# Attention values two units at a time, masks added by VectorE for half the batches, and a 64-row tail padded to 128 rows

## The chip, the cores and the metric

The kernel runs on one core of a Trainium2 chip. The metric is the device time of one execution in microseconds (us); lower is better. Each figure for a version is the median of several executions.

## The reference, cut to what matters

Three blocks follow each other, all in float32, on 4 batches of 576 positions and 512 features (8 heads of 64).

```python
scores = scale * np.matmul(q, k.transpose(0, 1, 3, 2))      # 4 x 8 x 576 x 576, D = 64
# heads 0-3: rel in [0, 32); heads 4-7: rel in [0, 128) and rel % 4 == 0
scores = np.where(masks, scores, -1e9); attn = softmax(scores)
x = (attn @ v) as (B, S, 512)
xk = mu_k * x + (1 - mu_k) * x_prev;  xr = mu_r * x + (1 - mu_r) * x_prev
x = sigmoid(xr @ w_r) * ((relu(xk @ w_k) ** 2) @ w_v)        # 512 -> 1024 -> 512
h = relu(x.T @ w_tok1) @ w_tok2                              # over positions: 576 -> 256 -> 576
u = x + h.T
out = u + relu(u @ w_ch1) @ w_ch2                            # 512 -> 1536 -> 512
```

## The kernel before, in words

**Attention.** The host cuts queries into blocks of 64 and gives each block the 96 keys that its window can reach (heads 4 to 7 are regrouped by position modulo 4, so that their window is one of 32 again). A unit is four such blocks, each for a pair of heads; a batch has 9 units, and there are 36. `attend` (line 542) does one unit. TensorE first writes the four masks (0 or -1e30, bf16) into a PSUM bank by one matmul with an identity (128x384), then adds four score matmuls (128x96, float32) on top. VectorE takes the negated maximum of each row, ScalarE makes the four exponentials from the bank, VectorE sums, inverts and scales them; TensorE transposes the four blocks, and one engine copies the result to `pt`. Then TensorE multiplies by the values: 8 matmuls of 96x64 by 96x64 that write 64 rows by 64 columns each, in the two halves of the array in turn. `nc.burst` (line 225) keeps these 8 together in the order. The result is copied to `xT`, where batch b lies in slots `xt` 4(b%3) to 4(b%3)+3.

**Gated block.** Six chunks of 384 positions. For each, `prep` makes the mixed inputs (high and low float32r parts, in `z` 0 to 3), `keys` and `mix` do 8 slices of the 1024 hidden features, and `receptance` the gate. A product of two float32 matrices is three float32r matmuls (`mm3`: high x high, high x low, low x high). The chunks' results are the tiles `x2`, 18 of 128 positions. A batch has four and a half such tiles; tiles 8 and 17 hold the last 64 positions of two batches, one in rows 0 to 63 and one in rows 64 to 127.

**Token mix.** `tokens_in(b)` (line 817) goes over the five tiles of a batch (`tiles_of`, line 807): it splits each into high and low (ScalarE or VectorE copies, VectorE subtracts) and multiplies by the weights `t1[kt]`, 6 matmuls of 512 columns per tile. For the fifth tile only the 64 rows of this batch are split and used, so its six matmuls have 64 rows: 24 in all. `t1[4]` holds the last 64 rows of `w_tok1` twice, once in each half of the rows. `tokens_out` multiplies by `t2` and adds to `u`. The channel mix (`middle`, `result`) ends the kernel.

**Weights.** `weight` (line 480) loads float64 words, and ScalarE and VectorE turn them into high and low parts: one pass of ScalarE, three of VectorE, then a copy and a subtraction. `t1`, `t2` and the first four slices of `w_ch1` go by turns through the two raw buffers `xt` 4 and 5 and the two work buffers `xt` 6 and 7 (`raw_b`, `tmp_b`); everything later goes through `wr` 0 to 2.

**Order.** No engine's order is written by hand. `Plan` records every operation, works out what it depends on, gives each a due time (`order`, line 280: the place of the matmuls in program order, counted back through what feeds them) and lists the operations by a schedule with costs per form. Line 392 issues them all, so every row of the profile bears this line, and rows are told apart by tiles: a tile bears the name of its slot (`at`, `x`, `xt`, `wk`, `wr`, `wv`, `z`, `y`, `cst`) without its number, `bank` is a PSUM bank. All DMAs are issued by SyncE (SP), in one order. Attention of batches 1 to 3 lies beside the gated block: `beside` (line 729) deals its units over the slices.

Of the kernel before, what the change touches and what calls it, by code (L numbers as in the profile page):

```python
# [10 lines left out]
F32R = mybir.dt.float32r  # L11
# [41 lines left out]
FIRST = [sum(TILES[:c]) for c in range(len(CHUNKS))]  # L53
CH = 512
NEG = -1.0e30

SLOTS = dict(
    cst=[160], xt=[584] * 12, x2=[2048] * 2 + [1024] * 5, at=[3536, 784, 1216],
# [347 lines left out]
def tile_model(nc, banks, units, cst, mu, w_k, w_v, w_r, w_t1, w_t2, w_c1, w_c2, outT):  # L406
    memory = {k: [Slot(f"{k}{i}", n) for i, n in enumerate(v)] for k, v in SLOTS.items()}

    def f(view):
        return view.bitcast(F32)  # L410
# [10 lines left out]
    def cut(name, numbers, size, count=None):  # L421

        out = []
        for n in numbers:
            out += [(name, n, size * i) for i in range(SLOTS[name][n] // size)]
        return out[:count]

    def ring(*places):
        return Ring(at, sum((p if isinstance(p, list) else [p] for p in places), []))
# [19 lines left out]
    def split(raw, hi, lo):  # L449
        copy(hi, raw)  # L450
        combine(lo, raw, f(hi), ALU.subtract)

    def rows(n):
        return slice(128 * n, 128 * n + 128)
# [6 lines left out]
    def pair(place, shape):  # L461

        name, number, offset = place
        n = int(np.prod(shape))
        return at(place, shape, F32R), at((name, number, offset + n), shape, F32R)
# [11 lines left out]

        return words(w).rearrange("(k p) c -> p k c", p=128)[:, :, 2 * n * m:2 * n * m + 2 * n]

    def weight(srcs, hi, lo, raw_ring, tmp_ring):  # L480

        shape = tuple(hi.shape[1:])
        n = int(np.prod(shape))  # L490
        flat = raw_ring.tile(2 * n, dtype=U32)
        for part, src in srcs:
            dst = flat[part]
            if len(src.shape) == 3:
                dst = dst.split(src.shape[1], src.shape[2])
            nc.sync.dma_start(out=dst, in_=src)
            if raw_ring is raw_a:
                nc.early[len(nc.ops) - 1] = 6
        raw = flat.split(n, 2)
        low, h = raw[:, :, 0], raw[:, :, 1]  # L500
        t = tmp_ring.tile(n)
        b, half = t.bitcast(U32), t.bitcast(U16)
        v = nc.vector
        nc.scalar.activation(out=t, in_=f(h), func=AF.Copy, scale=2.0 ** -112)
        v.tensor_scalar(out=h, in0=b, scalar1=3, scalar2=None, op0=ALU.logical_shift_left)
        v.scalar_tensor_tensor(
            out=b, in0=b, scalar=0x80000000, in1=h, op0=ALU.bitwise_and, op1=ALU.bitwise_or
        )
        v.scalar_tensor_tensor(
            out=half, in0=low, scalar=2.0 ** -29, in1=half, op0=ALU.mult, op1=ALU.add  # L510
        )
        if len(shape) == 2:
            t = t.split(*shape)
        split(t, hi, lo)
# [27 lines left out]
    def attend(i, s_ring, t_ring, x_ring):  # L542

        b, runs = UNITS[i]
        unit, vs = unit_r.tile(UQ + UK), v_r.tile(NBLK, 2, D)[:KB]
        values = units[i][:KB, UQ + UK:].rearrange("p (a b c) -> p a b c", a=NBLK, b=2)
        for out, in_ in ((unit, units[i][:, :UQ + UK]), (vs, values)):
            nc.sync.dma_start(out=out, in_=in_)
            nc.early[len(nc.ops) - 1] = {0: 30, 1: -45}.get(b, 0)
        blocks, o = [], UQ  # L550
        for p, j0, n in runs:
            if j0 == 0:
                nc.gpsimd.memset(out=xT[b, p][:, 0:1], constant=0.0)
            blocks += [(p, j0 + j, unit[:, o + QB * j:o + QB * j + KB]) for j in range(n)]
            o += QB * n + W
        sp, sm, st = s_ring.tile(NBLK, KB), sm_r.tile(NBLK, KB), st_r.tile(4, NBLK)
        row = ROWS[i % len(RUNS)]
        nc.tensor.matmul(out=sp, lhsT=ident_h, rhs=masks[:, row:row + NBLK, :], start=True, stop=False)
        for n, (p, j, ks) in enumerate(blocks):
            qs = unit[:, 2 * QB * n:2 * QB * n + 2 * QB]  # L560
            nc.tensor.matmul(out=sp[:, n, :], lhsT=qs, rhs=ks, start=False, stop=n == NBLK - 1)
            if b:
                nc.early[len(nc.ops) - 1] = -0.5 * n
        scale = 1.0 / np.sqrt(D)
        nc.vector.tensor_reduce(
            out=st[:, 0, :], in_=sp, axis=mybir.AxisListType.X, op=ALU.max, negate=True
        )
        if b == 0 and i % 2:
            nc.vector.tensor_tensor(out=sm, in0=sp, in1=st[:, 0, :].wide(KB), op=ALU.add)
            nc.scalar.activation(out=sm, in_=sm, func=AF.Exp, scale=scale)  # L570
            nc.vector.tensor_reduce(out=st[:, 2, :], in_=sm, axis=mybir.AxisListType.X, op=ALU.add)
        else:
            nc.either(
                ("vector", "tensor_scalar", dict(
                    out=st[:, 1, :], in0=st[:, 0, :], scalar1=scale, scalar2=None, op0=ALU.mult)),
                ("scalar", "activation", dict(out=st[:, 1, :], in_=st[:, 0, :], func=AF.Copy, scale=scale)),
            )
            for j in range(NBLK):
                nc.scalar.activation(
                    out=sm[:, j, :], in_=sp[:, j, :], func=AF.Exp, scale=scale,  # L580
                    bias=st[:, 1, j:j + 1], accum_out=st[:, 2, j:j + 1],
                )
        nc.either(
            ("vector", "tensor_scalar_add", dict(out=st[:, 2, :], in0=st[:, 2, :], scalar1=1e-9)),
            ("scalar", "activation", dict(out=st[:, 2, :], in_=st[:, 2, :], func=AF.Copy, bias=1e-9)),
        )
        nc.vector.reciprocal(out=st[:, 3, :], in_=st[:, 2, :])
        combine(sm, sm, st[:, 3, :].wide(KB), ALU.mult)
        tp, pt = t_ring.tile(NBLK, 2 * QB)[:KB], pt_r.tile(NBLK, 2 * QB)[:KB]
        for j in range(NBLK):  # L590
            nc.tensor.transpose(out=tp[:, j, :], in_=sm[:, j, :], identity=ident)
        copy(pt, tp)
        xp = x_ring.tile(QB * NBLK)
        start = len(nc.ops)
        for j in range(NBLK):
            for hh in range(2):
                r = slice(64 * hh, 64 * hh + 64)
                nc.tensor.matmul(
                    out=xp[r, QB * j:QB * j + QB], lhsT=vs[:, j, hh, :], rhs=pt[:, j, r],
                    start=True, stop=True,  # L600
                )
        nc.burst(start)
        o = 0
        for p, j0, n in runs:
            x, t, end = xT[b, p][:, 1:], QB * j0, QB * (j0 + n)
            if p < 2:
                copy(x[:, t:end], xp[:, o:o + end - t])
                o += end - t
                continue
            x = x.split(S // 4, 4).swap()  # L610
            while t < end:
                c, k = divmod(t, S // 4)
                m = min(end - t, S // 4 - k)
                copy(x[:, c, k:k + m], xp[:, o:o + m])
                t, o = t + m, o + m
# [108 lines left out]

    s_ring, t_ring, x_ring = psum(0, 4), psum(1), psum(2)
    unit_r = ring([("at", 0, (UQ + UK) * i) for i in range(2)])
    v_r = ring([("at", 0, 2 * (UQ + UK) + UV * i) for i in range(3)])
    beside = {}
    for n, (lo, hi) in enumerate(([0, 20], [20, 42], [42, 68])):
        for i in range(n_units):  # L730
# [35 lines left out]
            attend(h, s_ring, t_ring, x_ring)  # L766


    t1 = [pair(p, (HID,)) for p in cut("at", (1, 2), 512) + [("at", 0, 4 * S), ("at", 0, 4 * S + 512)]]
    t2 = [pair(p, (S,)) for p in cut("at", (0,), 2 * S, 2)]  # L770
    raw_b, tmp_b = ring(cut("xt", (4, 5), 512)), ring(cut("xt", (6, 7), 512))
    for k in range(4):
        weight([(everything, words(w_t1)[rows(k), :])], *t1[k], raw_b, tmp_b)
    tail = words(w_t1)[512:576, :]
    weight([(slice(0, 64), tail), (slice(64, 128), tail)], *t1[4], raw_b, tmp_b)
    for k in range(2):
        for n in range(3):
            cs = slice(192 * n, 192 * n + 192)
# [27 lines left out]

    def tiles_of(b):
        base, odd = 9 * (b // 2), b % 2
        out = [(base + 4 * odd + i, slice(0, 128), i) for i in range(4)]
        return out + [(base + 8, slice(64 * odd, 64 * odd + 64), 4)]  # L810

    for m in range(4):
        weight_1(m)
    hid = {}
    hp_r, x2p_r, up_r = psum(0, 1, 2, 3), psum(4, 5), psum(6, 7)

    def tokens_in(b):
        hp = [hp_r.tile(C) for _ in range(2)]
        for n, (t, r, kt) in enumerate(tiles_of(b)):
            h, l = x2h_r.tile(C, dtype=F32R), x2l_r.tile(C, dtype=F32R)  # L820
            split(x2[t][r], h[r], l[r])
            for m in range(2):
                mm3(hp[m], t1[kt][0][r, rows(m)], t1[kt][1][r, rows(m)], h[r], l[r], n == 0, n == 4)
        hid[b] = []
        for m in range(2):
            h, l = (hid_r.tile(C, dtype=F32R) for _ in range(2))
            nc.scalar.activation(out=h, in_=hp[m], func=AF.Relu)
            nc.vector.scalar_tensor_tensor(
                out=l, in0=hp[m], scalar=0.0, in1=f(h), op0=ALU.max, op1=ALU.subtract
            )  # L830
            hid[b].append((h, l))
# [189 lines left out]
```

## Time and profile before

| what | value |
|---|---|
| time, median of 3 runs | 734.55 us (733.45 to 735.19) |
| the profiled execution's own time | 732.79 us |
| its span, first to last instruction | 731.0 us |
| TensorE matmuls (PE) busy | 715.6 us, 98% of the span |
| VectorE (DVE) busy | 404.7 us, 55% |
| ScalarE (ACT) busy | 287.1 us, 39% |
| mean granted TensorE clock | 0.989 of full |
| moved by DMA | 53.84 MB, 74 GB/s |

PE is busy nearly all the time, but a matmul's busy time overlaps the next one's, so what a matmul costs is read from the distance between the starts of neighbours, not from its own duration. A float32 matmul counts as two rows of the trace (two passes), a float32r or bf16 one and a transpose as one.

### The profile page before, as it was taken

How to read it: one execution, taken by the hardware profiler on the slowest of the kernel's cores; microseconds unless marked ns; L12 is line 12 of the kernel's file. 1: busy time of each engine (PE TensorE's matmuls, PEld its weight loads, DVE VectorE, ACT ScalarE, POOL GpSimd, SP SyncE). 2: the span in 40 equal slices, each digit the busy share in tenths (PEclk: the TensorE clock that was granted, in tenths of full speed). 3: DMA queues.
4: the chain of work that ended last, by engine and by line, in shares of the span. 5: the costliest groups of instructions: out<-in, count | busy, mean ns of one | idle time of the engine just before them, and what ended most of it. 6: DMA issues, size and time to landing. Idle time of an engine off the chain costs nothing.

```text
span 731.0 us, 10615 instructions
## 1 busy us (share of the span) xinstructions
PE 715.6 (98%) x4124; PEld 604.6 (83%) x4124; DVE 404.7 (55%) x917; ACT 287.1 (39%) x803; POOL 1.2 (0%) x20
## 2 busy tenths in 40 slices
PE   7699999999999999999999999999999999999998
PEld 6578888888888888988878888888888888888897
DVE  6898898387477388786788898132114112211121
ACT  5776775356244354464466543120112011011110
POOL 0000000000000000000000000000000000000000
PEclk9799999999999999999999999999999999999999
DMA  8946632214122100203321342001000000100010
GB/s 293 323 156 225 196 132 81 67 52 144 47 68 70 46 16 22 73 30 105 98 81 54 96 127 76 1 0 58 1 0 23 35 1 1 57 1 0 1 59 30
DMA packets 26082, 53.84 MB, mean 74 GB/s; under 512 B 2480, under 2 KB 10032, under 8 KB 26032
## 3 DMA queue, kind: packets, MB, share of 16 engines
q1 hardware_dynamic: 26032, 53.17, 22.9%
q8 instruction: 32, 0.52, 0.3%
q14 instruction: 18, 0.15, 0.1%
HBM read 48.44 MB, written 4.72 MB: 73 GB/s over the span
## 4 chain that ended last, share of the span: by engine, by line
PE 95%; DMA 4%; SPq 0%; issue 0%; DVE 0%
PE bank L392 95%; DMA at<-units 2%; DMA wr<-units 1%; DMA wv<-units 1%; SPq L392 0%; DVE z L392 0%
## 5 line engine op out<-in xcount | busy, mean ns | idle before, releaser
L392 PE MATMUL bank<-z,wk 128*128 128x384 f32 (+2 forms) x816 | 196.4, 358 | 0.0
L392 DVE SCALAR_TENSOR_TENSOR z<-bank,z 128x512 fp32r<-128x512 f32 (+2 forms) x116 | 70.4, 607 | 222.3 <-ACT z L392 221.5
L392 ACT ACTIVATE z<-bank 128x512 fp32r<-128x512 f32 (+3 forms) x123 | 65.0, 529 | 285.3 <-PE bank L392 284.3
L392 PEld LDWEIGHTS bank<-z,wk 128*128 128x128 f32 x816 | 146.9, 188 | 15.1 <-ACT x L392 0.3
L392 PE MATMUL bank<-wv,z 128*128 128x512 f32 x432 | 128.9, 405 | 0.0
L392 PE MATMUL bank<-z,x 128*128 128x512 f32 (+1 forms) x540 | 120.2, 371 | 0.0
L392 PEld LDWEIGHTS bank<-z,x 128*128 128x128 f32 x540 | 94.9, 188 | 18.7
L392 PEld LDWEIGHTS bank<-wv,z 128*128 128x128 f32 x432 | 78.3, 189 | 13.8
L392 PE MATMUL bank<-z,at 128*128 128x512 f32 (+2 forms) x300 | 76.9, 388 | 0.0
L392 PE MATMUL bank<-wr,z 128*128 128x512 f32 x216 | 62.8, 406 | 0.0
L392 PEld LDWEIGHTS bank<-z,at 128*128 128x128 f32 (+1 forms) x300 | 52.6, 188 | 11.3 <-issue 1.3
L392 PE MATMUL bank<-at 128*128 128x96 f32 (+1 forms) x252 | 46.3, 284 | 11.0 <-DMA at<-cst 4.9
L392 ACT ACTIVATE at<-bank,at 128x96 f32<-128x96 f32 x128 | 42.4, 340 | 23.7 <-PE bank L392 11.6
L392 DVE TENSOR_TENSOR z<-z,z 128x384 fp32r<-128x384 f32 x88 | 48.1, 554 | 5.8 <-ACT z L392 2.6
L392 PE MATMUL bank<-xt,wk 128*128 128x512 f32 (+2 forms) x176 | 45.2, 387 | 0.0
L392 PEld LDWEIGHTS bank<-wr,z 128*128 128x128 f32 x216 | 39.2, 189 | 6.6
L392 PEld LDWEIGHTS bank<-at 128*128 128x128 f32 x216 | 35.3, 195 | 8.0 <-DMA at<-units 4.1
L392 PE MATMUL bank<-at,z 128*128 128x288 f32 x192 | 35.9, 306 | 0.0
L392 PEld LDWEIGHTS bank<-xt,wk 128*128 128x128 f32 x176 | 30.5, 192 | 6.1
L392 ACT ACTIVATE z<-z 128x384 fp32r<-128x384 f32 x57 | 29.5, 522 | 14.3 <-DVE z L392 8.3
L392 ACT ACTIVATE x<-bank 96x512 f32<-96x512 f32 (+1 forms) x41 | 24.2, 594 | 27.1 <-PE bank L392 26.9
L392 PEld LDWEIGHTS bank<-at,z 128*128 128x128 f32 x192 | 29.7, 188 | 4.0 <-issue 1.8
(106 smaller groups left out, 787.2 us busy)
## 6 DMA issues: line engine op xcount, KB each, us to landing
at<-units SPq DMA_DIRECT2D x27, 416.0 KB, 3.7
wr<-w_c SPq DMA_DIRECT2D x20, 512.0 KB, 3.6
at<-units SPq DMA_DIRECT2D x27, 192.0 KB, 2.6
x<-w_k SPq DMA_DIRECT2D x4, 1024.0 KB, 6.9
x<-w_v SPq DMA_DIRECT2D x4, 1024.0 KB, 7.0
wv<-units SPq DMA_DIRECT2D x8, 416.0 KB, 6.6
outT<-z SPq DMA_DIRECT2D x9, 256.0 KB, 2.0
x<-w_r SPq DMA_DIRECT2D x4, 512.0 KB, 3.6
```

The source lines that it names most:

```text
L392: call(kw["out"], kw["constant"]) if method == "memset" else call(**kw)
```

## The change

Three edits and what they need.

1. For batches 2 and 3 (18 of the 36 units) the mask matmul is gone. The four score matmuls open their own sums, VectorE adds the mask while it moves the scores from the bank to the tile `sm`, and maximum and exponentials read `sm`.
2. The value matmuls of batches 1 to 3 are done for two units in one burst of 16 (the ninth unit of a batch stays alone): `attend` puts a unit on the list `waiting`, and `weigh` does what waits and copies it out by `place`. The ring of value tiles has a fourth place (`y`).
3. The fifth tile of a batch is used with all its 128 rows. The last 64 rows of `w_tok1` are prepared twice: `t1[4]` has them in rows 0 to 63 and zeros below, `t1[5]` (in `z512[8]`, which lies in slot `z` 2) the other way round; GpSimd (POOL) writes the zeros into the raw words. The tile is split once for both batches and its parts stay in `wr` 3.

```diff
+MASKED = 2
+TOGETHER = 2
...
-    def weight(srcs, hi, lo, raw_ring, tmp_ring):
+    def weight(srcs, hi, lo, raw_ring, tmp_ring, zero=None):
...
+        if zero is not None:
+            nc.gpsimd.memset(out=f(flat[zero]), constant=0.0)
...
-        nc.tensor.matmul(out=sp, lhsT=ident_h, rhs=masks[:, row:row + NBLK, :], start=True, stop=False)
+        mask = masks[:, row:row + NBLK, :]
+        by_pe = b < MASKED
+        if by_pe:
+            nc.tensor.matmul(out=sp, lhsT=ident_h, rhs=mask, start=True, stop=False)
...
-            nc.tensor.matmul(out=sp[:, n, :], lhsT=qs, rhs=ks, start=False, stop=n == NBLK - 1)
+            nc.tensor.matmul(out=sp[:, n, :], lhsT=qs, rhs=ks, start=not by_pe, stop=n == NBLK - 1 or not by_pe)
...
+        if not by_pe:
+            nc.vector.tensor_tensor(out=sm, in0=sp, in1=mask, op=ALU.add)
+            sp = sm
...
-        xp = x_ring.tile(QB * NBLK)
+        waiting.append((runs, b, vs, pt))
+        if b == 0 or len(waiting) == TOGETHER or (i + 1) % len(RUNS) == 0:
+            weigh(x_ring.tile(2, QB * NBLK))
+    def weigh(xps):
         start = len(nc.ops)
...
+        for n, (_, _, vs, pt) in enumerate(waiting):
+            for j in range(NBLK):
...
         nc.burst(start)
+        for n, (runs, b, _, _) in enumerate(waiting):
+            place(runs, b, xps[:, n, :])
+        waiting.clear()
...
-    v_r = ring([("at", 0, 2 * (UQ + UK) + UV * i) for i in range(3)])
+    v_r = ring([("at", 0, 2 * (UQ + UK) + UV * i) for i in range(3)], ("y", 0, 0))
...
-    weight([(slice(0, 64), tail), (slice(64, 128), tail)], *t1[4], raw_b, tmp_b)
+    halves = [slice(0, 64), slice(64, 128)]
+    for odd in range(2):
+        weight([(halves[odd], tail)], *t1[4 + odd], raw_b, tmp_b, zero=halves[1 - odd])
...
-        out = [(base + 4 * odd + i, slice(0, 128), i) for i in range(4)]
-        return out + [(base + 8, slice(64 * odd, 64 * odd + 64), 4)]
+        return [(base + 4 * odd + i, i) for i in range(4)] + [(base + 8, 4 + odd)]
...
-            h, l = x2h_r.tile(C, dtype=F32R), x2l_r.tile(C, dtype=F32R)
-            split(x2[t][r], h[r], l[r])
+            elif b % 2 == 0:
+                h, l = ends[b // 2] = at(("wr", 3, 0), (C,), F32R), at(("wr", 3, 512), (C,), F32R)
+            else:
+                h, l = ends[b // 2]
+            if n < 4 or b % 2 == 0:
+                split(x2[t], h, l)
...
-                mm3(hp[m], t1[kt][0][r, rows(m)], t1[kt][1][r, rows(m)], h[r], l[r], n == 0, n == 4)
+                mm3(hp[m], t1[kt][0][:, rows(m)], t1[kt][1][:, rows(m)], h, l, n == 0, n == 4)
```

The change moves nothing by hand, but the schedule is made anew, so rows shift on every engine. Three places matter.

**TensorE, beside the gated block.** Before, a unit of batch 2: a mask (the weight load of `at_0_98` and the 128x384 matmul from it), the burst of one unit (64x64 x8) and scores (128x96) among the gated block's rows.

```order
L392 MATMUL bank_64<-z_0_580,wk_0_421 128x384 x3
L392 MATMUL bank_65<-wr_1_589,z_0_434 128x512 x2
L392 LDWEIGHTS at_0_98
L392 MATMUL bank_61<-at_0_98 128x384
L392 MATMUL bank_63<-x_0_188,at_0_333 64x64 x8
L392 MATMUL bank_61<-at_0_333 128x96 x2
L392 MATMUL bank_65<-wr_1_589,z_0_434 128x512
```

And a like place of the changed kernel:

```order
L394 MATMUL bank_61<-at_0_333 128x96
L394 MATMUL bank_65<-z_0_463,wk_0_330 128x384 x4
L394 MATMUL bank_66<-wv_1_987,z_1_569 128x512
L394 MATMUL bank_63<-x_0_188,at_0_333 64x64 x16
L394 MATMUL bank_66<-wv_1_987,z_1_569 128x512 x2
L394 MATMUL bank_67<-wv_1_987,z_1_569 128x512 x3
```

The mask's two rows are gone, and 16 value matmuls stand in one row. In all, the value matmuls stood in 34 unbroken runs and now stand in 23 (in batch 0 two units happen to follow each other in both).

**VectorE, the same units, changed kernel.** `at1_0_98` holds the masks, `at2_0_133` is `sm`.

```order
L394 TENSOR_TENSOR at2_0_133<-bank0_61,at1_0_98 128x384
L394 TENSOR_TENSOR z1_0_553<-z5_0_494,z1_0_553 128x384
L394 TENSOR_TENSOR at2_0_133<-at2_0_133 128x384
L394 TENSOR_REDUCE at2_0_133<-at2_0_133 128x4
L394 SCALAR_TENSOR_TENSOR z5_0_494<-xt3_0_73,cst0_0_95,z5_0_494 128x128
L394 TENSOR_SCALAR at2_0_133<-at2_0_133 128x4
```

The first row is new; the maximum (128x4) now reads `sm` where it read the bank.

**SP, the loads of the token mix's weights.** Before, the two raw buffers `xt4` and `xt5` take turns:

```order
L392 DMA xt4_0_83<-w_t1 64x512 x2
L392 DMA xt5_0_85<-w_t2 128x384
L392 DMA xt4_0_83<-w_t2 128x384
L392 DMA xt5_0_85<-w_t2 128x384
L392 DMA xt4_0_83<-w_t2 128x384
L392 DMA xt5_0_85<-w_t2 128x384
L392 DMA xt4_0_83<-w_t2 128x384
L392 DMA xt5_0_85<-w_c1 128x2x256
```

In the changed kernel:

```order
L394 DMA xt4_0_85<-w_t1 64x512
L394 DMA xt5_0_83<-w_t1 64x512
L394 DMA xt4_0_85<-w_t2 128x384
L394 DMA xt5_0_83<-w_t2 128x384
L394 DMA xt4_0_85<-w_t2 128x384 x2
L394 DMA xt4_0_85<-w_c1 128x2x256 x4
L394 DMA wr2_2_3096<-w_c1 128x4x256
L394 DMA wr0_2_3112<-w_c2 128x1024
L394 DMA wr1_2_3128<-w_c2 128x1024
L394 DMA xt5_0_83<-w_t2 128x384 x2
```

`xt4` runs ahead to its four half slices of `w_ch1`, and `xt5` stands with one piece of `w_tok2` until after the first loads into `wr`: two more pieces of `w_tok2`, and behind these rows four half slices of `w_ch1`, come later than they did.

## Rows read from the trace of the kernel before

**Rows 1.** The page: span, and the line of PE in its part 1.

```profile
span 731.0 us, 10615 instructions
PE 715.6 (98%) x4124; PEld 604.6 (83%) x4124; DVE 404.7 (55%) x917; ACT 287.1 (39%) x803; POOL 1.2 (0%) x20
```

**Rows 2.** The chain that ended last, from 29.70 us on: start us, us, what.

```profile
29.70 50.45 PE bank L392 x352
...
80.16 647.21 PE bank L392 x3601
```

**Rows 3.** Timeline of PE: start us, us, engine, line, operation, out<-in, shape, count.

```profile
142.89 0.85 PE L392 MATMUL bank<-wr,z 128*128 128x512 f32 x3
143.67 0.69 PE L392 MATMUL bank<-x,at 96*64 96x64 f32 x16
144.28 0.74 PE L392 MATMUL bank<-wr,z 128*128 128x512 f32 x2
144.86 0.34 PE L392 MATMUL bank<-at 128*128 128x384 bf16 x1
144.90 0.53 PE L392 MATMUL bank<-wr,z 128*128 128x512 f32 x1
145.26 0.36 PE L392 MATMUL bank<-at 128*128 128x96 f32 x2
```

**Rows 4.** Timeline of PE, in the first attention: two units' values in succession.

```profile
40.03 0.69 PE L392 MATMUL bank<-x,wr 96*64 96x64 f32 x16
40.54 0.64 PE L392 MATMUL bank<-x,z 96*64 96x64 f32 x16
41.11 3.49 PE L392 MATMUL bank<-xt,wk 128*128 128x384 f32 x10
```

**Rows 5.** Timeline of PE in the token mix: rows with 128 rows of weights.

```profile
412.27 0.29 PE L392 MATMUL bank<-at,z 128*128 128x288 f32 x1
412.40 1.31 PE L392 MATMUL bank<-z,at 128*128 128x512 f32 x5
413.56 0.29 PE L392 MATMUL bank<-at,z 128*128 128x288 f32 x1
```

**Rows 6.** The same view: half tiles; the first row merges two full and four half ones.

```profile
379.85 1.76 PE L392 MATMUL bank<-z,at 128*128 128x512 f32 x6
381.54 0.54 PE L392 MATMUL bank<-at,z 128*128 128x288 f32 x2
382.00 0.50 PE L392 MATMUL bank<-z,at 64*128 64x512 f32 x1
382.43 0.40 PE L392 MATMUL bank<-at,z 128*128 128x288 f32 x1
382.76 0.50 PE L392 MATMUL bank<-z,at 64*128 64x512 f32 x1
383.19 1.19 PE L392 MATMUL bank<-at,z 128*128 128x288 f32 x7
```

**Rows 7.** Groups by form: xcount | busy us, mean ns of one | idle before, releaser.

```profile
L392 PE MATMUL bank<-z,at 64*128 64x512 f32 x24 | 8.8, 444 | 0.0
L392 DVE TENSOR_TENSOR at<-at 128x384 f32<-128x384 f32 x36 | 19.8, 553 | 0.2
L392 ACT ACTIVATE x<-bank 96x512 f32<-96x512 f32 x24 | 14.2, 594 | 11.8 <-PE bank L392 11.5
L392 DVE SCALAR_TENSOR_TENSOR xt<-xt,xt 128x256 uint16<-128x256 uint32 x13 | 5.6, 450 | 0.2
L392 DVE SCALAR_TENSOR_TENSOR xt<-xt,xt 128x192 uint16<-128x192 uint32 x6 | 2.2, 377 | 0.0
L392 POOL MEMSET xt<- 128x1 f32 x16 | 1.1, 111 | 57.1 <-PE bank L392 56.8 <-POOLq L1005 0.3
```

**Rows 8.** Windows: stretch, its us, busy us (instructions) of each engine, PE clock, DMA.

```profile
100.00:250.00 150.00, 150.00 (x1022) 128.46 (x1022) 98.46 (x250) 72.02 (x246) 0.00 (x0) 1.00 0.26 74
356.00:430.00 74.00, 74.00 (x422) 61.91 (x421) 63.68 (x120) 45.18 (x101) 0.00 (x0) 1.00 0.26 81
```

More of the change, by code (lines that the diff above doesn't have):

```diff
@@ L592, in attend, with place @@
         copy(pt, tp)
-        xp = x_ring.tile(QB * NBLK)
-        start = len(nc.ops)
[L595 to L601, printed above, removed]
+        waiting.append((runs, b, vs, pt))
+        if b == 0 or len(waiting) == TOGETHER or (i + 1) % len(RUNS) == 0:
+            weigh(x_ring.tile(2, QB * NBLK))
+    waiting = []
+    def weigh(xps):
+        start = len(nc.ops)
+        for n, (_, _, vs, pt) in enumerate(waiting):
+            for j in range(NBLK):
+                for hh in range(2):
+                    r = slice(64 * hh, 64 * hh + 64)
+                    nc.tensor.matmul(
+                        out=xps[r, n, QB * j:QB * j + QB], lhsT=vs[:, j, hh, :], rhs=pt[:, j, r],
+                        start=True, stop=True,
+                    )
         nc.burst(start)
+        for n, (runs, b, _, _) in enumerate(waiting):
+            place(runs, b, xps[:, n, :])
+        waiting.clear()
+    def place(runs, b, xp):
         o = 0
@@ L766, in tile_model @@
             attend(h, s_ring, t_ring, x_ring)
-    t1 = [pair(p, (HID,)) for p in cut("at", (1, 2), 512) + [("at", 0, 4 * S), ("at", 0, 4 * S + 512)]]
+    t1 = [pair(p, (HID,)) for p in cut("at", (1, 2), 512) + [("at", 0, 4 * S), ("at", 0, 4 * S + 512), z512[8]]]
     t2 = [pair(p, (S,)) for p in cut("at", (0,), 2 * S, 2)]
@@ L808, in tiles_of @@
         base, odd = 9 * (b // 2), b % 2
-        out = [(base + 4 * odd + i, slice(0, 128), i) for i in range(4)]
-        return out + [(base + 8, slice(64 * odd, 64 * odd + 64), 4)]
+        return [(base + 4 * odd + i, i) for i in range(4)] + [(base + 8, 4 + odd)]
     for m in range(4):
         weight_1(m)
-    hid = {}
+    hid, ends = {}, {}
     hp_r, x2p_r, up_r = psum(0, 1, 2, 3), psum(4, 5), psum(6, 7)
@@ L818, in tokens_in @@
         hp = [hp_r.tile(C) for _ in range(2)]
-        for n, (t, r, kt) in enumerate(tiles_of(b)):
-            h, l = x2h_r.tile(C, dtype=F32R), x2l_r.tile(C, dtype=F32R)
-            split(x2[t][r], h[r], l[r])
+        for n, (t, kt) in enumerate(tiles_of(b)):
+            if n < 4:
+                h, l = x2h_r.tile(C, dtype=F32R), x2l_r.tile(C, dtype=F32R)
+            elif b % 2 == 0:
[4 more added lines that the diff above has]
+                split(x2[t], h, l)
             for m in range(2):
-                mm3(hp[m], t1[kt][0][r, rows(m)], t1[kt][1][r, rows(m)], h[r], l[r], n == 0, n == 4)
+                mm3(hp[m], t1[kt][0][:, rows(m)], t1[kt][1][:, rows(m)], h, l, n == 0, n == 4)
         hid[b] = []
```

## The prediction

> **What bounds the kernel now.** I read the page first [rows 1]: PE is busy 715.6 of 731.0 us. A busy share of 98% need not mean that PE sets the end, so the chain of waits comes next [rows 2]: from 29.70 us it is PE alone, 50.45 us and then 647.21 us without another engine or a wait in between. So from 29.7 us on, a us that PE no longer needs is a us less, as long as nothing that feeds PE becomes late. The question is what the removed rows cost PE, and whether VectorE, ScalarE or SP are near enough to take PE's place. The cost of a row on PE is read from the starts of its neighbours in the timeline.
>
> **Two scales.** Durations come from the profiled execution: 732.79 us, a span of 731.0 us and 1.79 us around it. The median of the runs, 734.55 us, stands 1.76 us above that execution. I subtract from the median. A measurement of this kernel can tell about 0.2% (1.5 us) from no change.
>
> **The masks.** Between 144.86 and 145.26 us stand one mask matmul and one 512-column matmul [rows 3], 0.40 us. A 512-column matmul alone takes 0.232 us: five go by between 412.40 and 413.56 [rows 5]. The mask thus costs PE 0.17 us, and its weight load lies beside the matmul ahead. 18 masks go: 18 x 0.17 = 3.1 us. With the reading's rounding of 0.01 us the bounds are 2.9 and 3.2.
>
> In their place stand 18 additions of 128x384 on VectorE. No row shows one with a bf16 mask; the nearest are the 128x384 tensor_tensor from SBUF at 553 ns [rows 7], below it nothing and above it twice that. I take 0.55 us, 9.9 us in all. From 100 to 250 us, where most of them go, VectorE is busy 98.46 of 150 us [rows 8], so 51 us are free and even 20 us fit. I cost them at nothing; without that cover they would cost what the first rival below says. The maximum moves from the bank to `sm` at the same 384 columns, and 72 exponentials now read SBUF: ScalarE has 78 of 150 us free there.
>
> **The bursts.** From 142.89 to 144.86 us there are five 512-column matmuls and a burst of 8 [rows 3]: 1.97 - 5 x 0.232 = 0.81 us for the burst. Only 0.61 us of it lie between its start and the next row's; the rest is a late start after the row ahead (0.78 us for three matmuls that take 0.70) and a slow row behind (0.58 us for two that take 0.46). Two units that follow each other [rows 4] take 1.08 us from 40.03 to 41.11, and with the same 0.20 us outside 1.28, where two bursts apart take 1.62. Joining two saves 0.34 us; I hold 0.30 to 0.35 possible. The order shows 34 unbroken runs before and 23 now: 11 x 0.34 = 3.7 us, bounds 3.3 and 3.9. The array's work itself does not shrink: the same 288 matmuls are issued. In a pair the first unit's `xT` comes as late as the second's; every pair lies within one batch and is complete before the chunk that reads it, and the copies out of the bank are as many as before.
>
> **The half tile.** With 128 rows, a 512-column matmul takes 0.232 us and a 288-column one 0.13 us [rows 5]. From 381.54 to 383.19 us stand three of 288 and two half-tile matmuls [rows 6]: 1.65 us, where full rows would take 3 x 0.13 + 2 x 0.232 = 0.85. Each of the two pays 0.40 us over its columns: a late start, 0.43 us until the next row's start, and a slow row behind. The cost is one of entering and leaving: the first row of the group holds two full and four half tiles that follow each other, and its six take 1.69 us until the next start, 0.30 us over 6 x 0.232 and not four times that. The 24 [rows 7] stand in 12 unbroken runs, counted along the timeline: 12 x 0.40 = 4.8 us, bounds 4.3 and 5.0. With 128 rows they join the rows around them. Zero rows add nothing to the columns that are streamed.
>
> A page's rule would count this edit the other way. "TensorE: Matmul & The Clock Gate", section "Packing small matmuls" of the Trainium skill, says that matmuls on different row groups overlap in the array, so that a small-row matmul costs a few ns beside another; by it the edit would give up an overlap, and the sum would be 1.2 instead of 11.6 us. The trace disagrees: 0.43 us pass before the next row can start, since the rows around use all 128 rows.
>
> **What the half tile adds.** One more `weight` of 256 columns: three VectorE passes of up to 450 ns [rows 7] and a subtraction, at most 1.8 us, and two passes of ScalarE; against this two of four tail splits go. Two memsets of 64x512 words on POOL; the trace has only 128x1 at 111 ns [rows 7], so their price is open from 0.1 us up to many times that. POOL does nothing else then, and the load into the other half of the same buffer runs beside them. I take nothing; the bound is in the range.
>
> The odd tail's parts go to slot `z` 2, which the last chunk's gate still reads. Until then the work buffer `xt` 7 is held, and three pieces of `w_tok2` and four half slices of `w_ch1` queue behind it, as the order on SP shows. At four VectorE operations each, priced by their longest (377 and 450 ns [rows 7]), a piece of 192 columns costs at most 1.5 us and one of 256 at most 1.8: 3 x 1.5 + 4 x 1.8 = 11.7 us that can move from the gated block into the stretch from 356 to 430 us. There VectorE is busy 63.68 of 74 us [rows 8], and the stretch gets 4.8 us shorter. It fits only if other work goes out: the later slices of `w_ch1` and `w_ch2`, needed well after 430 us, can, and the new order does put them later. I cost it at nothing, and the second rival says what it costs otherwise.
>
> SP keeps the same bytes. Its first twenty loads stand as before, so the start up to 29.7 us stays.
>
> **Sum.** 3.1 + 3.7 + 4.8 = 11.6 us, by the bounds 10.5 to 12.1. 732.79 - 11.6 = 721.2 for an execution like the profiled one, and **734.55 - 11.6 = 722.95, say 723.0 us** for the median. With the runs' own spread of about 0.9 us each way this case gives 721.5 to 724.9.
>
> **The rivals.**
>
> *The added VectorE step shows.* Each unit of batches 2 and 3 is 0.55 us later, and if PE has nothing else to do at that moment it waits: 18 x 0.55 = 9.9 us back, 732.9 us. For it: PE's order is fixed. Against: the gated block's matmuls stand between scores and values everywhere, and PE waits for nothing after 29.7 us though the chain of a unit already has four VectorE steps.
>
> *VectorE fills up in the token mix.* If the 11.7 us that move in push nothing out, VectorE has 75.4 us of work in 69.2 us, and PE waits up to 6.2 us: 729.2 us at most. For it: VectorE is the busiest feeder in just that stretch. Against: part of its work there is for weights of a later stage and can give way.
>
> *The half tiles overlap after all.* By the rule above the 24 matmuls would be nearly free now and cost 24 x 0.232 = 5.6 us with 128 rows: 6.8 - 5.6 = 1.2 us saved, 733.3 us. Against it the 0.43 us [rows 6].
>
> *The pair makes PE wait, and the kernel gets slower.* A burst can start only when the second unit's transposes are copied to `pt`, one copy of 594 ns [rows 7] behind four transposes of about 0.11 us. There are two places of `pt` and one bank for the result, so nothing of a third unit can go ahead to hide it. If PE stood still at each of the 15 bursts of batches 1 to 3 for transposes and copy, 15 x 1.03 = 15.5 us: 738.4 us. It makes the kernel slower from (11.6 + 1.5) / 15 = 0.87 us a burst. Against it: single bursts need the same copy today and the chain shows no wait, and the order puts gated matmuls between.
>
> **How the numbers follow.** The forecast 0.78; VectorE filling up 0.12; the VectorE step showing 0.05; overlap 0.02; the pair waiting 0.03. The range runs from 721.2 to 728.0: past the forecast's own on both sides, and most of the way to the second rival's price, which is an upper bound. Faster: 0.78 + 0.12 and 0.01 of the 0.05, whose 732.9 lies just past the bound, 0.91. Same: the rest of that and the overlap, 0.06. Slower: 0.03.
>
> **What would show it.** Right: PE's chain again unbroken from about 29.7 us; bf16 matmuls x18; no 64*128 rows; the starts around an x32 burst some 0.34 us closer than around two; the gated block 5 to 7 us shorter and the token mix 4 to 5. Wrong: waits of PE for VectorE or ScalarE before bursts (first and fourth rivals), for `wv` or `z` from VectorE in the token mix (second), or padded 512-column rows that take longer than 0.232 us (third). A start later than 29.7 us would say that the new order moved a load that I took to stand still.

## The result and the profile after

| version | median us | of executions | lowest to highest |
|---|---|---|---|
| before | 734.87 | 4 | 733.45 to 735.40 |
| changed | 721.87 | 4 | 721.18 to 722.79 |

The ratio is 0.9827, 95% interval 0.9808 to 0.9846: 13.0 us faster, between 11.3 and 14.1. The forecast was 723.0 us with a range of 721.2 to 728.0. A second measurement of the same kernel, among the runs below, gave 721.51 us against 733.53 and a ratio of 0.9832, 0.9805 to 0.9859.

The page of the changed kernel has the same picture as [rows 1]: PE is busy for 98% of a shorter span, and VectorE and ScalarE each have some 5 us more.

```profile
span 721.0 us, 10581 instructions
PE 705.4 (98%) x4106; PEld 605.6 (84%) x4106; DVE 409.1 (57%) x927; ACT 292.6 (41%) x813; POOL 2.1 (0%) x22
```

The chain that ended last (start us, us, what) is again one of PE alone, but from 42.02 us instead of 29.70 [rows 2]; ahead of it stand loads of weights and their conversion, as far down as `keys`' weights in `wk`:

```profile
19.49 11.18 DMA x<-w_v
...
35.56 4.54 DMA x<-w_r
...
40.18 0.68 ACT x L394
40.86 0.95 ACT wk L394
41.81 0.20 issue
42.02 675.33 PE bank L394 x3851
```

PE's waits of the changed kernel (who waits for whom: us in total, times, longest) are all over by 42.02 us, so nothing in the gated block or the token mix waits:

```profile
PE bank L394 <- DMA at<-cst: 4.8, 1, 4.8
PE bank L394 <- DMA at<-units: 3.4, 1, 3.4
PE bank L394 <- ACT at L394: 2.8, 1, 2.8
PE bank L394 <- ACT wk L394: 0.4, 1, 0.4
PE bank L394 <- DVE xt L394: 0.4, 1, 0.4
```

The groups by form (xcount | busy us, mean ns of one | idle before): 18 masks are left of 36, and VectorE's 128x384 row from the bank stands 22 times, 4 of them as before and 18 new, at 556 ns. The memsets that I could not price take 525 ns.

```profile
L394 PE MATMUL bank<-at 128*128 128x384 bf16 x18 | 6.4, 392 | 7.6 <-DMA at<-cst 4.8 <-ACT at L394 2.8
L394 DVE TENSOR_TENSOR at<-bank,at 128x384 f32<-128x384 f32 x22 | 12.2, 556 | 13.8 <-PE bank L394 13.7
L394 POOL MEMSET xt<- 64x512 f32 x2 | 1.1, 525 | 222.0 <-ACT z L394 211.6 <-DVE xt L394 10.4
```

A joined burst in the timeline of PE: 0.33 us from the row ahead, 1.08 us to the next start, and eight 512-column matmuls behind it in 1.95 us.

```profile
165.83 0.40 PE L394 MATMUL bank<-wv,z 128*128 128x512 f32 x1
166.16 1.15 PE L394 MATMUL bank<-x,at 96*64 96x64 f32 x32
167.24 2.11 PE L394 MATMUL bank<-wv,z 128*128 128x512 f32 x8
169.19 2.24 PE L394 MATMUL bank<-z,wk 128*128 128x384 f32 x12
```

That is 0.33 + 1.08 + 1.95 - 9 x 0.232 = 1.27 us for two units, where I had 1.28. And the padded fifth tile, where [rows 6] had the half tiles:

```profile
374.97 0.43 PE L394 MATMUL bank<-at,z 128*128 128x288 f32 x2
375.24 0.40 PE L394 MATMUL bank<-wr,z 128*128 128x512 f32 x1
375.47 0.30 PE L394 MATMUL bank<-at,z 128*128 128x288 f32 x1
375.61 0.39 PE L394 MATMUL bank<-wr,z 128*128 128x512 f32 x1
375.83 1.36 PE L394 MATMUL bank<-at,z 128*128 128x288 f32 x9
```

From 374.97 to 375.83 us three matmuls of 288 and two padded ones of 512 columns take 0.86 us; the same five took 1.65 us.

**Two parts of every execution.** To compare kernels whose first 45 us differ, I split each profiled execution. *Rows*: for each PE row the usual distance from its start to the next one's, which is the median over all stretches past 80 us, in these runs, with the same forms ahead and behind; summed over the whole program, with what was in fact taken past 80 us in its place there. *Start*: the rest, which is PE's time before its first row, its waits, and rows at the lower of the two granted clocks (1.2 instead of 2.4 GHz; before and after, the clock is 0.50 of full from 30 to 35 us and 1.00 from 40 us on). Both end at the start of PE's last row. Some forms stand only in the first 80 us; how they are priced, and from which runs, moves the *rows* of all kernels by some us, and a difference in the third column by up to 0.6 us.

| kernel | rows us | against before | start us |
|---|---|---|---|
| before | 702.5 | | 24.6 |
| changed, first profile | 691.1 | -11.4 | 26.0 |
| changed, second profile | 690.8 | -11.7 | 26.2 |
| masks alone | 699.9 | -2.6 | 26.0 |
| padded tile alone | 697.9 | -4.6 | 24.5 |
| joined bursts alone | 698.4 | -4.1 | 26.6 |
| joined bursts, three value places | 698.4 | -4.1 | 25.2 |

PE's rows became 11.4 to 11.7 us cheaper, and the three edits add up: 2.6 + 4.6 + 4.1 = 11.3 us. The profiled executions of before and of the changed kernel differ by only 10.0 us: that of the changed kernel was the slowest of its four, and its start is 1.4 us longer.

### The profile page after: what moved, and what is told of

Read it like the earlier page. It is cut to its first block, busy times and chain, and to the rows that moved or that the text cites. A ratio compares the mean times of both kernels' runs of the same rounds, so it can differ in the third digit from the quotient of the medians.

```text
span 721.0 us, 10581 instructions
## 1 busy us (share of the span) xinstructions
PE 705.4 (98%) x4106; PEld 605.6 (84%) x4106; DVE 409.1 (57%) x927; ACT 292.6 (41%) x813; POOL 2.1 (0%) x22
## 4 chain that ended last, share of the span: by engine, by line
PE 94%; DMA 4%; DVE 0%; ACT 0%; SPq 0%; issue 0%; ACTq 0%
PE bank L394 94%; DMA x<-w_v 2%; DMA wr<-units 1%; DMA wv<-units 1%; DMA x<-w_r 1%; SPq L394 0%; DVE x L394 0%; ACT x L394 0%; ACT wk L394 0%; DVE at L394 0%; DVE z L394 0%; ACTq L394 0%
## 5 line engine op out<-in xcount | busy, mean ns | idle before, releaser
L394 PE MATMUL bank<-z,wk 128*128 128x384 f32 (+2 forms) x816 | 200.0, 358 | 0.0
L394 PE MATMUL bank<-z,at 128*128 128x512 f32 (+1 forms) x276 | 69.0, 383 | 0.0
L394 PE MATMUL bank<-wr,z 128*128 128x512 f32 x228 | 66.7, 404 | 0.0
L394 PEld LDWEIGHTS bank<-z,at 128*128 128x128 f32 x276 | 48.5, 188 | 8.6
L394 PE MATMUL bank<-at 128*128 128x96 f32 (+1 forms) x234 | 41.2, 277 | 11.0 <-DMA at<-cst 4.8
L394 PEld LDWEIGHTS bank<-wr,z 128*128 128x128 f32 x228 | 41.5, 188 | 6.9
L394 ACT ACTIVATE x<-bank 96x512 f32<-96x512 f32 (+1 forms) x45 | 26.8, 596 | 34.7 <-PE bank L394 34.3
L394 ACT ACTIVATE at<-at 128x96 f32<-128x96 f32 (+2 forms) x107 | 34.5, 325 | 9.0 <-DVE at L394 8.3
```

Of the source, the lines that this page charges most:

```text
L394: call(kw["out"], kw["constant"]) if method == "memset" else call(**kw)
```

## Experiments

**Each edit alone.** Three kernels, each the kernel before with one of the edits; their diffs are the matching parts of the diff above. Masks alone:

> The kernel before with the mask edit alone: 18 mask matmuls less, 18 additions of 128x384 on VectorE more. Its order has 35 unbroken runs of value matmuls where before has 34, one burst of the first batch standing apart. My theory (PE is the bound, the additions are hidden): 18 x 0.17 = 3.1 us less, and 0.34 us back for the run that came apart, about 2.8 us faster than before. Rival one (the addition shows): 9.9 - 3.1 = 6.8 us slower than before if every addition is exposed, about no change if a third of them is. Rival two (only the profiled pair's difference counts, 5.5 us for masks and bursts together instead of 6.8): about 2.2 us faster.

Measured 730.06 us against 733.58 (22 executions of before), ratio 0.9957, 0.9941 to 0.9972: 3.5 us faster, 2.1 to 4.3. The rows are 2.6 us cheaper. The rival that the addition shows is out; 2.8 us and rival two's 2.2 can't be told apart here.

Padded tile alone:

> The kernel before with the padded fifth tile alone (mask matmuls for all batches, every unit's values in a burst of its own). My theory (a half-tile run costs 0.40 us for entering and leaving): 12 x 0.40 = 4.8 us faster than before, all of it between about 370 and 435 us. Rival (half tiles had overlapped with their neighbours, by the rule on different row groups): 24 x 0.232 = 5.6 us slower. Rival (VectorE fills up in the token mix): less than 4.8 us faster, by waits of PE for VectorE there, down to 1.4 us slower.

Measured 727.99 us, ratio 0.9925, 0.9907 to 0.9943: 5.6 us faster, 4.2 to 6.8; the rows 4.6 us. The chain of PE starts at 29.49 us (before 29.70) and runs for 693.18 us. It has no wait for VectorE in the token mix.

Joined bursts alone:

> The kernel before with the joined value bursts alone (batches 1 to 3, masks by matmul, half tiles as they were). Its order has 22 unbroken runs of value matmuls where before has 34. My theory: 12 x 0.34 = 4.1 us faster. Rival one (PE waits for the second unit's transposes and copy): 15 x 1.03 = 15.5 us back, 11.4 us slower. Rival two (most of the 0.34 us was only read into the late and slow neighbours): 12 x 0.10, from the 0.51 us between the starts of two adjacent bursts against 0.61 us to the next row, so about 1.2 us faster.

Measured 731.13 us, ratio 0.9968, 0.9954 to 0.9983: 2.5 us faster, 1.2 to 3.4. That misses 4.1 us, and yet the rows are 4.1 us cheaper and no burst past 70 us waits (the last wait of PE, 0.3 us, ends at 69.06 us and is for a piece of `w_v` that ScalarE converts). What is missing is in the start, 26.6 us instead of 24.6. SP's timeline of this run (start us, us, what):

```profile
34.36 0.33 SPq L394 DMA_DIRECT2D x<-w_r  x1
34.73 0.90 SPq L394 DMA_DIRECT2D at<-units  x2
35.67 0.43 SPq L394 DMA_DIRECT2D y<-units  x1
39.04 6.84 SPq L394 DMA_DIRECT2D x<-w_r  x2
45.97 0.38 SPq L394 DMA_DIRECT2D at<-units  x1
47.68 0.33 SPq L394 DMA_DIRECT2D x<-w_r  x1
```

Three value loads stand between the first and the second load of `w_r`, and a unit's load ahead of the fourth, where before one value load stood behind the first and none ahead of the others. The timeline shows where that reaches PE: ScalarE stands idle for 2.20 us until the second `w_r` has landed, behind it stand the copies into `xt`, and PE waits 1.68 us for these. In the kernel before, ScalarE does not wait for `w_r` there.

```profile
43.74 0.66 ACT L394 ACTIVATE x<-x 128x512 f32<-128x512 f32 x1 [2.20 <-DMA x<-w_r]
44.82 3.46 PE L394 MATMUL bank<-xt,wk 128*128 128x384 f32 x10 [1.68 <-ACT xt L394]
```

**The fourth value place.** The same kernel, with the ring of value tiles as it was:

```diff
-    v_r = ring([("at", 0, 2 * (UQ + UK) + UV * i) for i in range(3)], ("y", 0, 0))
+    v_r = ring([("at", 0, 2 * (UQ + UK) + UV * i) for i in range(3)])
```

> The kernel with the joined value bursts alone, but with the three places of before for the value tiles instead of four. The number of value runs stays 22. Its order of loads has no load into the fourth place; there the run with four places issues it ahead of the second load of w_r. Theory (PE's rows get 4.1 us cheaper, and what the first run of this edit lacked, 2.45 instead of 4.1 us by the medians, is a start made later by value loads that stand ahead of w_r): without the fourth place the loads of w_r come about one load of 192 KB earlier, some 0.6 us, and the time is 0.3 to 1 us below the run with four places, about 730.4 us. Rival (the fourth place is what keeps the pair from waiting): PE waits for value loads at bursts past 60 us, and the time is above that of the run with four places, by up to 15 bursts of a load's 5 us.

Measured 729.23 us against 733.24, ratio 0.9948, 0.993 to 0.9966: 4.0 us faster than before, 2.5 to 5.1. It points the way the theory said (rows the same, start 25.2 us), but the interval overlaps that of the run with four places. In the trace ScalarE waits 1.11 instead of 2.20 us for the second `w_r`, and PE 0.66 instead of 1.68 us for the copies behind it. The rival is out: with three places nothing past 60 us waits. The same edit on the changed kernel:

> The changed kernel with the three places of before for the value tiles. Theory (the fourth place gives PE nothing and costs at the start one load of 192 KB ahead of the second w_r): equal to the changed kernel or up to 0.6 us faster, 721.0 to 721.8 us. Rival (the place hides loads of values behind the joined bursts): waits of PE for loads past 60 us and a slower kernel.

Measured 722.15 us, ratio 0.9839, 0.9824 to 0.9855: no difference from the changed kernel. So the fourth place is neither needed nor a cost there, and what it costs at the start of the kernel with joined bursts alone is seen in one trace of each, some 1 us of PE's waits, but not in the times.

**The addition twice.**

```diff
             nc.vector.tensor_tensor(out=sm, in0=sp, in1=mask, op=ALU.add)
+            nc.vector.tensor_tensor(out=sm, in0=sm, in1=mask, op=ALU.add)
```

> The changed kernel with each of the 18 mask additions done twice on VectorE (the mask is added a second time to the tile; masked scores become -2e30, the softmax is the same): 18 x about 0.55 = 9.9 us more work on VectorE, nothing else. If the additions are hidden behind PE, as I costed them: no change against the changed kernel, about 722 us. If they are exposed: 9.9 us slower than the changed kernel, about 732 us, and then the first additions already take that much from the change. If a part is exposed, that part of 9.9.

Measured 721.47 us, ratio 0.9836, 0.9814 to 0.9858. The added rows are there, and PE's chain has as many rows and the same length as without them (675.33 us):

```profile
L394 DVE TENSOR_TENSOR at<-at,at 128x384 f32<-128x384 f32 x18 | 10.0, 553 | 0.2
```

```profile
41.53 675.23 PE bank L394 x3851
```

So 10.0 us of additions more, one more step in the chain of 18 units, cost nothing that shows, and the first 18 additions nothing either. VectorE's total rose by only 2.4 us, from 409.1 to 411.5, because the order gave other work away: ScalarE is busy 298.1 us here and 292.6 without them.

**Masks of a third batch by VectorE.**

```diff
-MASKED = 2
+MASKED = 1
```

> The changed kernel with the masks of batch 1 by VectorE too: 9 mask matmuls less, 9 additions of 0.55 us more, of which most fall between 50 and 130 us, where VectorE is busy 45 of 50 us in the changed kernel from 50 to 100 us. The order has 22 unbroken value runs instead of 23. If VectorE still has room: 9 x 0.17 + 0.34 = 1.9 us faster than the changed kernel, about 719.8 us. Rival (VectorE is full there): 4 to 5 us more of its work in a stretch with 5 us free, PE waits for VectorE between 50 and 110 us, and the gain is lost, up to about 3 us slower than the changed kernel.

Measured 720.84 us against 733.24, ratio 0.9832, 0.9813 to 0.9851: not to be told from the changed kernel. The rows are 1 us cheaper, the start is 27.6 us, the longest of all. The first three waits of PE, all before 42 us:

```profile
PE bank L394 <- DMA at<-cst: 5.4, 1, 5.4
PE bank L394 <- ACT x L394: 4.2, 2, 3.8
PE bank L394 <- ACT wk L394: 2.2, 1, 2.2
```

The rival's price between 50 and 110 us did not come: PE stands still there once, for 0.08 us. But VectorE is full, as the rival said: it is busy 9.92 of the 10 us from 100 to 110 us (8.82 in the changed kernel), and the chain that ended last is PE's alone only from 109.88 us on. From 89.99 us it goes over VectorE, a load of `w_v` and its conversion:

```profile
108.69 1.14 DVE wv L394
109.88 608.12 PE bank L394 x3366
```

So by this run the third batch uses up VectorE's room in this place. This run doesn't tell whether its order or a slow start by chance made the waits for weights before 42 us.

**Half tiles beside half tiles.** The rule that I turned down in the prediction is tried where it could hold: the 12 half-tile matmuls of two batches in one burst, alternating between the row halves.

```diff
...
+            for m in range(2):
+                for k, (w, x) in enumerate(((0, h), (0, l), (1, h))):
+                    for odd, r in enumerate(halves):
+                        nc.tensor.matmul(
+                            out=ends[b + odd][m], lhsT=t1[4][w][r, rows(m)], rhs=x[r],
+                            start=k == 0 and odd == 1, stop=k == 2 and odd == 0,
+                        )
+            nc.burst(start)
...
```

What is left out (`...`) puts the last 64 rows of `w_tok1` back once into each half and splits the tile once.

> The changed kernel with another fifth tile: the last 64 rows of the weights stand once in each half of the rows, as before the change, the tile is split once with 128 rows, and its 12 matmuls for the two batches stand in one burst that changes between rows 0 to 63 and rows 64 to 127 at every matmul and between two banks; two such bursts in all, no zero rows, no memsets. If matmuls on different row groups overlap in the array (the Trainium skill's rule in the page on TensorE and the clock gate, section on packing small matmuls): a burst takes 6 x 0.232 = 1.4 us and 0.40 us for entering and leaving, 1.8 instead of 12 x 0.232 = 2.8 us, so 2.0 us faster than the changed kernel, about 719.7 us. If they do not overlap: 12 x 0.232 and 0.40 us, 0.8 us slower than the changed kernel, about 722.5 us. If every change of row group costs what entering and leaving cost (0.40 us a matmul): 2 x 12 x 0.40 = 9.6 us slower.

Measured 719.85 us against 733.24, ratio 0.9811, 0.9796 to 0.9826. That is 1.7 and 2.0 us below the changed kernel's two measurements (each beside a before of its own); all four executions (718.93 to 720.40 us) lie below all nine of these (720.73 to 722.79), while the intervals of the ratios overlap. Its rows are 689.5 us, 1.3 to 1.6 less, with one wait of 0.3 us for VectorE at 390.78 us in them that the changed kernel does not have. Timeline of PE:

```profile
362.38 0.38 PE L394 MATMUL bank<-cst,x 128*128 128x128 f32 x2
362.69 1.66 PE L394 MATMUL bank<-wr,at 64*128 64x512 f32 x12
364.29 0.87 PE L394 MATMUL bank<-cst,x 128*128 128x128 f32 x6
```

Twelve matmuls of 512 columns in 1.60 us, where one after the other they need 2.78. In the trace their starts stand in six pairs, 1 to 10 ns apart within a pair. They do run at once.

The yardstick for the last three runs, on their chip:

> The changed kernel once more, unchanged, beside the three that follow on the same chip, as their yardstick. Theory (PE's work is 11.0 us less, and the executions differ by their first 45 us): 721.3 to 722.3 us against a before of 732.5 to 734.5 us, a difference between 11 and 13 us.

Measured 721.51 us against 733.53, ratio 0.9832, 0.9805 to 0.9859: 12.0 us.

**Does the alternation matter?**

```diff
-                for k, (w, x) in enumerate(((0, h), (0, l), (1, h))):
-                    for odd, r in enumerate(halves):
+                for odd, r in enumerate(halves):
+                    for k, (w, x) in enumerate(((0, h), (0, l), (1, h))):
```

> The kernel of the run with alternating half tiles, the same 24 matmuls in the same two bursts, but in another order: three matmuls on rows 0 to 63, then three on rows 64 to 127, and again. Theory (two matmuls run at once only where neighbours in the order use different rows): three pairs of twelve still meet, so a burst takes 9 x 0.232 instead of 6 x 0.232 us; 2 x 0.70 = 1.4 us slower than the alternating order, about 0.6 us faster than the changed kernel. Rival (the array takes any two matmuls of different rows from a window, in whatever order): as fast as the alternating order, and the trace shows the same 1.6 us a burst. Rival (rows of 64 are just faster, overlap or not): the same 1.6 us as well, but with starts 0.13 us apart rather than in pairs.

Measured 720.33 us, ratio 0.9815, 0.9788 to 0.9841. My theory fell, by the trace and not by the time, which lies between the theory and the rivals: the burst is as short as the alternating one, and its starts stand in six pairs too, 8 to 17 ns apart. The third matmul of the program, which signals that its bank is done, stands fifth among the starts, at 362.34 us: the fourth and the fifth of the program started ahead of it.

```profile
361.77 1.67 PE L394 MATMUL bank<-wr,at 64*128 64x512 f32 x12
363.37 0.87 PE L394 MATMUL bank<-cst,x 128*128 128x128 f32 x6
```

**The ninth unit too.**

```diff
-        if b == 0 or len(waiting) == TOGETHER or (i + 1) % len(RUNS) == 0:
+        if b == 0 or len(waiting) == TOGETHER or i + 1 == len(UNITS):
```

> The kernel with alternating half tiles, and the value bursts joined across batches too: the ninth unit of batches 1 and 2 goes with the first unit of the next batch. Its order has 22 unbroken runs of value matmuls instead of 23. Theory (0.34 us for each run that goes): 0.3 us faster than the kernel with alternating half tiles, about 2.2 us faster than the changed kernel. Rival (the ninth unit's values come too late for the chunk that reads them, since its partner is dealt to a later slice): waits of PE for copies into xt or for the mixed inputs in z between 100 and 230 us, and slower.

Measured 719.99 us, ratio 0.9821, 0.979 to 0.9851; rows 689.3 us, 0.2 less than without. No wait was added past 60 us but one of 0.3 us in the token mix that the kernel with alternating half tiles has too. 0.3 us is too little to be seen in the times.

**Do column halves overlap as well?**

```diff
-            for j in range(NBLK):
-                for hh in range(2):
+            for hh in range(2):
+                for j in range(NBLK):
```

> The changed kernel with the value matmuls of a unit in another order: four that write rows 0 to 63 of the bank, then four that write rows 64 to 127, where the changed kernel changes sides at every matmul. Theory (matmuls on the two column halves of the array do not overlap here: eight in two passes of 64 columns take 0.51 us in a run, 16 x 64 / 2400 = 0.43 us one after the other, half of that if they overlapped): no change, within 0.5 us, or faster by what a change of side costs. Rival (they do overlap in part): each of the 36 units pays up to 0.2 us more, up to 7 us slower, the units of batches 1 to 3 in full, 27 x 0.2 = 5.4 us.

Measured 728.41 us, ratio 0.9928, 0.9904 to 0.9952: 6.9 us slower than the changed kernel beside it, for an order within bursts alone. The rival is right. The burst that answers to the one at 166.16 us above:

```profile
168.45 0.40 PE L394 MATMUL bank<-wv,z 128*128 128x512 f32 x1
168.77 1.54 PE L394 MATMUL bank<-x,at 96*64 96x64 f32 x32
170.24 2.11 PE L394 MATMUL bank<-wv,z 128*128 128x512 f32 x8
```

1.47 instead of 1.08 us, 0.195 us a unit; 36 units make 7.0 us. The value matmuls have run two at a time all along: in the kernel before as in the changed one their starts stand in pairs, 7 ns apart.

## Why the prediction was right, point by point

**What bounds the kernel.** Right. PE's chain is unbroken to the end, and the time fell by what PE's rows became cheaper. The gated block ends 5.2 us earlier than before, by its last row with `wv`, and the token mix is 4.9 us shorter, from there to its last 288-column row; 5 to 7 and 4 to 5 were forecast. I said that a start later than 29.7 us would mean a moved load. The chain starts at 42.02 us, but not for that reason alone: `x<-w_v` was issued at 17.98 us before and at 19.49 us after, behind the same loads in the same order, and the first rows that wait for a load into `at` start at 29.70 us before, 31.77 in the changed kernel, and 29.49 to 31.62 in runs of single edits. The start differs by some 2 us between executions whose first twenty loads are equal. The kernel of the last run, with the two column halves one after the other, has all its loads in the changed kernel's order, and its chain starts at 29.91 us. Behind the first twenty the order did change from before to the changed kernel, but towards less: ahead of the first load of `w_r` stand three value loads of 192 KB, where two and a unit's 416 KB stood. So the pace of the loads, not a moved one, is what the start of the changed kernel shows; in the kernel with the joined bursts alone moved loads are there as well. I looked at twenty loads; the four of `w_r`, for which the first stage waits too, stand behind them.

**The masks.** 18 x 0.17 = 3.1 us: measured 2.6 us of rows, with one value run more (0.34 us) that the order pulled apart; together 2.9 us. The addition costs 0.556 us each and none of it is seen, which the doubled one shows.

**The bursts.** 0.34 us for each run joined: measured 4.1 us for 12, that is 0.34; priced in other ways the rows give 3.5 to 4.6 us, 0.29 to 0.38. Reading the late neighbour and the slow one as part of the burst's price was what made it right; from the distance of its own starts alone, 0.61 twice against 1.08 us, it would have been 0.14.

**The half tile.** 12 x 0.40 = 4.8 us: measured 4.6 by rows. Padding costs nothing, as said: a padded row takes 0.23 us to the next start (375.24 to 375.47 us).

**The rule turned down.** The number was right and the reason was half wrong. I wrote that the trace disagrees with the rule in "TensorE: Matmul & The Clock Gate", section "Packing small matmuls" of the Trainium skill. It does not: the half tiles of [rows 6] stood between rows that use all 128 rows of the array, and there the rule gives no overlap to lose. With half tiles beside each other the rows bear it out: the two of a pair start 1 to 10 ns apart, and the kernel is 1.3 to 2.0 us faster than with the padding. These 1.3 to 2.0 us are what the prediction did not see.

**Work moved behind slot `z` 2.** VectorE is busy 67.89 us from 356 to 430 us, 63.68 before, and PE waits for nothing there. These are not the same rows of the program, since the changed kernel is ahead by then: what lay from 356 to 430 us lies from 350.8 to 419.9 us, and there VectorE is busy 62.89 of 69.1 us, less than before and not the 75.4 us of the rival. So other work gave way.

```profile
100.00:250.00 150.00, 150.00 (x1062) 132.71 (x1061) 103.82 (x265) 83.12 (x286) 0.00 (x0) 1.00 0.26 79
356.00:430.00 74.00, 74.00 (x439) 65.81 (x438) 67.89 (x134) 47.09 (x106) 0.00 (x0) 1.00 0.31 95
```

In these windows of the changed kernel (columns as in [rows 8]) VectorE has 5.4 us more from 100 to 250 us and ScalarE 11.1: the additions went to VectorE, and operations that either engine can do moved to ScalarE, which has 40 more there.

**The size.** Forecast 11.6 us, measured 13.0 (11.3 to 14.1) and again 12.0. The rows give 11.4 to 11.7. What the first measurement shows beyond that lies for the most part in its before: 734.87 us from 4 executions, where the other measurements of the same kernel, from 22, 11 and 11, have 733.58, 733.24 and 733.53. Against these the changed kernel is some 12 us faster. My 734.55, the median of 3, was high by the same 1 us, and that is why the forecast time was 1.1 us too long while the forecast gain was not.

## What to carry to other kernels

Where one engine's chain is unbroken, price an edit by what it does to the distance between the starts of neighbours, the late row ahead and the slow row behind included. A narrow matmul among full ones pays for entering and leaving, here 0.40 us a run: pad it, or better, put narrow ones of the other half of the array beside it, and they run two at a time. Before calling a start unchanged, follow the order of loads to the last weight that the first stage waits for.

## What the runs showed of the hardware that was not expected

Matmuls on two halves of the array run at once, on row halves (512 columns each, pairs 0.23 us apart) and on column halves (two passes of 64 columns). The second half does not need to be the next row of the program: with three matmuls on one row half ahead of three on the other, they still paired, 1.60 us for twelve. The page of the Trainium skill named above says in the same section that matmuls start and end in program order; for the starts that run speaks against it. But the reach is short. In the kernel that writes a unit's four matmuls on one column half ahead of the four on the other, a burst of two units stands like this in the timeline (`y` holds the first unit's values, `at` the second's):

```profile
154.74 0.79 PE L394 MATMUL bank<-x,y 96*64 96x64 f32 x13
155.31 0.27 PE L394 MATMUL bank<-x,at 96*64 96x64 f32 x1
155.37 0.22 PE L394 MATMUL bank<-x,y 96*64 96x64 f32 x1
155.42 0.22 PE L394 MATMUL bank<-x,at 96*64 96x64 f32 x1
155.43 0.22 PE L394 MATMUL bank<-x,y 96*64 96x64 f32 x1
155.48 0.22 PE L394 MATMUL bank<-x,at 96*64 96x64 f32 x1
155.48 0.22 PE L394 MATMUL bank<-x,y 96*64 96x64 f32 x1
155.54 0.74 PE L394 MATMUL bank<-x,at 96*64 96x64 f32 x13
156.21 0.97 PE L394 MATMUL bank<-z,wk 128*128 128x384 f32 x4
```

The second unit's first row starts at 155.31 us, ahead of three rows of the first unit that stand before it in the program, and from there they start beside each other. Where the same half stands eight rows (four matmuls of two passes) in succession, as it does here, the first four rows of the burst start alone, 107 and then 58 ns apart, and pairs form only from the fifth on. So the partner was found three or four rows ahead in the program and not five to eight. That is a reading of starts in two kernels, not a limit that was measured, and what sets it is open.
